# Turning 128 tokens' activations by DMA instead of on TensorE, in a fused attention and feed-forward kernel

## The chip, the cores and the metric

The kernel runs on one core of one Trainium2 chip. A core has five engines that run their own instruction lists side by side: PE (TensorE, matrix products into PSUM), DVE (VectorE), ACT (ScalarE), POOL (GpSimd) and SP (SyncE, which here only issues transfers). Sixteen DMA engines move data between HBM and the on-chip memory SBUF. The metric is device time of one execution in microseconds (us), as the median of several runs.

## The reference

Eight batches, twelve heads, 448 tokens, head size 64; the attention has no softmax, and its output is the input of a two-layer network with squared ReLU:

```python
scores = scale * np.matmul(q, k.transpose(0, 1, 3, 2))
attn = np.maximum(scores, 0.0) ** 2 / S
x = np.matmul(attn, v)          # rearranged to 3584 tokens x 768
h = x @ w_in                    # 768 -> 2048
g = np.maximum(h, 0.0) ** 2
out = g @ w_out                 # 2048 -> 768
```

## The kernel before

Everything on the chip is in fp16, with fp32 sums in PSUM. The attention is cut into 24 units (8 batches, 3 groups of 4 heads). Per unit and 64-key round, PE makes scores (L525), DVE or ACT takes the ReLU out of PSUM (`rel`, L541 on DVE, L544 on ACT), ACT or POOL squares it (`at`, L548 and L551), and PE multiplies by v (`av`, L591). When a batch's three units are done, the attention output stands turned in `xt` (L611, L613), and PE multiplies it by w_in (L653): the result `h` comes with the hidden features on the partitions, so that its square, `g` (ACT L642, masked by DVE L637), can be the stationary operand of the products with w_out (L873).

The products with w_out are a two-by-two Strassen scheme (`o_groups`): two chunks of 128 tokens, and the two halves of w_out in both directions, give seven products of eight matmuls instead of eight. It needs sums of g (`s1` to `s4`, buffers `comb`, DVE L852), sums of w_out (`t1` to `t4`, buffers `wt` and one of `w`, DVE L839), and partial results (`part`: copies by ACT L793 or DVE L795, closing sums by DVE L885, then stores by SP, L749). In the order of the code the seven are called m1, m2, m6, m5, m7, m3, m4. m1 and m2 read g itself, of the first chunk; m6 needs s2 and t2; m5 needs s1 and t1; m4 reads g of the second chunk. s2 is made from s1, and t2 from t1.

The first batch is started early, in two parts: its first 128 tokens, then the other 320. For the first 128 (`h_first`), PE multiplies the other way round (L702, four groups of six matmuls, one for each quarter of w_in as it arrives), so that the result has the tokens on the partitions. ACT squares (L715) and DVE masks it (L710) into two `comb` buffers. Then, twice, eight PE transposes (L729) turn it into PSUM, and a copy by ACT or DVE (L732) brings it into `g`. The tokens 0 to 127 of batch 0 are `chunk(0, 0)`; they are paired with `chunk(0, 1)` in the first seven products, while `chunk(0, 2)` waits for `chunk(1, 0)` of the next batch.

Loads: POOL issues w_in (L499), v (L492), the first q and k (L409) and w_out (L504); SP issues the later q and k (`raw`, L392), each held back by a one-element POOL memset (L389) on its buffer. From the seventh unit on, q and k are cast by POOL (L443) and turned by transposing DMAs from SP (L479); before that, PE turns them (L463, copies L466).

No order is written down. Each operation is given to a planner (`Plan`) with its cost on each engine that could do it, its inputs, its buffers and a due time; the planner plays the program through with those costs, tries a few rules, keeps the order that ends first by its own reckoning, and emits the instructions of each engine in that order. `after` holds an operation back in the planner's time alone: on the chip an engine goes on as soon as its semaphores allow. While PE has nothing ready before planner time 45, the planner gives it dummy matmuls (L1023) to keep it busy. A POOL operation that follows one of the L839 or L852 operations in the plan waits for it.

The lines that place the work around the change:

```python
work += [(0.2157 * NM, wide(z, 2 * two + z)) for z in range(2)]
work.append((0.057 * NH, turn))
...
new = o_groups(chunk(0, 0), chunk(0, 1))
push([(0.0, combine_w2)])
...
new = o_groups(chunk(b - 1, 2), chunk(b, 0))
```

Of the kernel before, what the change touches and what calls it, by code (L numbers as in the profile page):

```python
# [11 lines left out]
FP16 = mybir.dt.float16  # L12
# [288 lines left out]
def kernel(  # L301
# [9 lines left out]
    nc = tc.nc  # L311
# [7 lines left out]
    P = 128  # L319
# [6 lines left out]
    NH = NF // 2  # L326
# [7 lines left out]
    sb = ctx.enter_context(tc.tile_pool(name="sb", bufs=1))  # L334
    psum = ctx.enter_context(tc.tile_pool(name="ps", bufs=1, space=bass.MemoryType.PSUM))

    def fixed(pool, name, n, shape, dt):
        return [pool.tile(shape, dt, name=f"{name}{i}", tag=f"{name}{i}") for i in range(n)]
# [4 lines left out]
    ident = sb.tile([P, P], FP16, name="ident", tag="ident")  # L343
# [6 lines left out]
        "xt": fixed(sb, "xt", 2, [P, NM, S], FP16),  # L350
        "g": fixed(sb, "g", 2, [P, NF, S], FP16),
        "rest": fixed(sb, "rest", 2, [P, NF, P], FP16),
        "comb": fixed(sb, "comb", 6, [P, NH, P], FP16),
        "part": fixed(sb, "part", 6, [P, HALF], FP32),
        "rel": fixed(sb, "rel", 8, [P, 512], FP32),
        "mm": fixed(psum, "mm", 8, [P, 512], FP32),
# [1 line left out]
    plan = Plan(pools, {"PE": 5.0, "ACT": 0.7, "DVE": 1.2, "POOL": 1.4, "SP": 0.7})  # L358
# [10 lines left out]
    def act(n, emit):  # L369
        return "ACT", 0.09 + 0.00081 * n, 0.187 + 0.00081 * n, emit  # L370

    def dve(n, emit):
        return "DVE", 0.07 + 0.001045 * n, 0.149 + 0.001045 * n, emit
# [135 lines left out]
    PARTS = slice(0, 2 * TP), slice(2 * TP, S)  # L509
# [150 lines left out]
    def h_group(b, f):  # L660
        def run():
            gts.setdefault(b, Buf("g"))
            bank = Buf("mm")
            op = plan.pe(0.1892 * NM, h_mms(bank, b, f, WHOLE, 0),
                         xt_ops[b, 0] + [w1_ops[f // 4]], [bank, xts[b]])
            evac_g(op, bank, b, [f], WHOLE)
        return 0.1892 * NM, run

    def h_part(fs, cols):

        w = cols.stop - cols.start
        cost = max(0.098, 0.000424 * w) * NM
        cell: list = []

        def block(z):
            def run():
                gts.setdefault(0, Buf("g"))
                if not z:
                    cell.append(Buf("mm"))
                op = plan.pe(cost, h_mms(cell[0], 0, fs[z], cols, z * w),  # L680
                             xt_ops[0, cols.start] + [w1_ops[fs[z] // 4]] + cell[1:],
                             [cell[0], xts[0]])
                cell.append(op)
                if z == len(fs) - 1:
                    evac_g(op, cell[0], 0, fs, cols)
            return run

        return [(cost, block(z)) for z in range(len(fs))]

    def h_first():  # L690

        work = []
        for two in range(2):
            buf, marks = Buf("comb"), []

            def wide(z, i, buf=buf, marks=marks):
                def run():
                    bank = Buf("mm")

                    def emit():  # L700
                        for m in range(NM):
                            nc.tensor.matmul(  # L702
                                bank.tile, lhsT=xts[0].tile[:, m, PARTS[0]], rhs=w1[i][:, m, :],
                                start=(m == 0), stop=(m == NM - 1), skip_group_check=True)

                    def dst():
                        return buf.tile[:, 4 * z:4 * z + 4].rearrange("p f c -> p (f c)")

                    def mask():
                        nc.vector.scalar_tensor_tensor(  # L710
                            out=dst(), in0=bank.tile, scalar=0.0, in1=dst(), op0=ALU.is_gt,
                            op1=ALU.mult)

                    op = plan.pe(0.2157 * NM, emit, xt_ops[0, 0] + [w1_ops[i]], [bank, xts[0]])
                    one = plan.add([act(512, lambda: nc.scalar.activation(  # L715
                        out=dst(), in_=bank.tile, func=AF.Square))], [op], [bank, buf],
                        due=plan.now + 0.3)
                    marks.append(plan.add([dve(512, mask)], [one], [bank, buf],
                                          due=plan.now + 0.9))
                return run  # L720

            def turn(two=two, buf=buf, marks=marks):
                gts.setdefault(0, Buf("g"))
                ps, g = Buf("mm"), gts[0]

                def flip():
                    flat = ps.tile.bitcast(FP16)
                    for f in range(NH):
                        nc.tensor.transpose(flat[:, f * P:(f + 1) * P], buf.tile[:, f], ident)  # L729

                def copy(fn):
                    return lambda: fn(  # L732
                        g.tile[:, NH * two:NH * two + NH, PARTS[0]],
                        ps.tile.bitcast(FP16).rearrange("p (f c) -> p f c", c=P))

                op = plan.pe(0.057 * NH, flip, list(marks), [ps, buf])
                done = plan.add(
                    [("DVE", 0.62, 0.7, copy(nc.vector.tensor_copy)),
                     ("ACT", 0.93, 1.02, copy(nc.scalar.copy))], [op], [ps, g],
                    due=plan.now + 0.3)  # L740
                g_ops.setdefault(0, []).append((done, two, PARTS[0]))

            work += [(0.2157 * NM, wide(z, 2 * two + z)) for z in range(2)]
            work.append((0.057 * NH, turn))
        return work

# [15 lines left out]
    def filled(b, half, cols):  # L762

        return [op for op, h, c in g_ops[b]
                if half in (None, h) and c.start < cols.stop and cols.start < c.stop]
# [13 lines left out]
    def chunk(b, c):  # L779
        cols = slice(c * P, (c + 1) * P)  # L780
        return (lambda half=None: filled(b, half, cols), lambda: gts[b], lambda: gts[b].tile[:, :, cols],
                [(b, 2 * c), (b, 2 * c + 1)])

    def rest_chunk(pr):
        return (lambda half=None: rests[pr][0], lambda: rests[pr][1], lambda: rests[pr][1].tile,
                [(2 * pr, TJ - 1), (2 * pr + 1, TJ - 1)])
# [151 lines left out]
    def push(work):  # L938
        nonlocal queued
        for c, fn in work:  # L940
            fifo.append((c, fn))
            queued += c
# [13 lines left out]
    def push_dense(b):  # L956
        if b:
            hs = [h_group(b, f) for f in range(NF)]
        else:
            hs = [z for f in range(NF) for z in h_part([f], PARTS[1])]  # L960
        if b == 0:
            if PLAIN0:
                both = [plain_groups(chunk(b, c)) for c in range(2)]
                new = [both[c][hf] for hf in range(2) for c in range(2)]
            else:
                new = o_groups(chunk(0, 0), chunk(0, 1))
                push([(0.0, combine_w2)])
        elif b % 2 == 0:
            new = o_groups(chunk(b, 0), chunk(b, 1))
        else:  # L970
            pr = b // 2
            new = o_groups(chunk(b - 1, 2), chunk(b, 0))
            if pr % 2 == 1:
                new += o_groups(rest_chunk(pr - 1), rest_chunk(pr))
            new += o_groups(chunk(b, 1), chunk(b, 2))
        old = backlog[:QUOTA[b]]
        beside = max(0, len(old) - 2)
        done = 0
        for i, g in enumerate(hs):
            push([g])  # L980
            upto = (i + 1) * beside // len(hs)
            push(old[done:upto])
            done = upto
        if b == 0:
            push([(0.0, lambda: None)])
        if b % 2 == 1:
            push([(0.0, lambda: rest(b // 2))])
        push(old[done:])
        backlog[:] = backlog[len(old):] + new
        now = QUOTA[b] - len(old)  # L990
        push(backlog[:now])
        del backlog[:now]
        if b == 0 and PLAIN0:
            push([(0.0, combine_w2)])

    ORDER = "u3 v3 u4 v4 u5 v5 w0 w2 w3 w1"
    EARLY = 6
    PLAIN0 = False
    NPE = 6
    FIRST = (((21,), None), ((22, 23), None), ((24, 25), None), ((26, 27), None), ((28, 29), None),  # L1000
             (range(30, 34), 3), ((34, 35), None), ((36, 37), None), (range(38, 42), 4))
# [104 lines left out]
    for w_ in "kq":  # L1106
        turn_pe(3, w_, casts[3, w_])
    some_h(NF)
    push_dense(0)

    def coming(n):
# [10 lines left out]
    for steps, done in bursts():  # L1122
        now = steps[0] if steps else ROUNDS
        for n in range(NU, NUN):
# [6 lines left out]
            if n > 3 and reached("turn", n, TJ * (n - 1) - 5):  # L1131
                if n >= EARLY:
                    for w in "kq":
                        casts[n, w] = cast_qk(n, w, raws[n, w])
                if n < NPE:
                    for w in "kq":
# [22 lines left out]
        if done is not None and done % NU == NU - 1:  # L1159
            push_dense(done // NU)  # L1160
# [36 lines left out]
```

## Time and profile before

| | us |
|---|---|
| median of 13 runs | 379.31 (378.05 to 381.95) |
| the profiled execution | 379.53 |
| its span, first to last instruction | 377.8 |
| PE busy in the span | 367.0 |
| DVE, ACT, POOL busy | 272.7, 269.4, 221.0 |

The span leaves 1.73 us of the execution's time around it. Times in the profile count from the start of the span. A line such as "PE mm L653" is the group of PE instructions of line 653 of the kernel that write the buffers `mm`. "Busy" for PE contains modelled ends of pipelined matmuls, so neighbouring pieces overlap a little; in the chain of waits the pieces follow each other without overlap, and they are the ones to add up.

### The profile page before, as it was taken

The numbers are of one execution on the slowest core, as the hardware profiler recorded it, in microseconds if no ns is written. First come the engines' busy times: TensorE is split into PE (matmuls) and PEld (weight loads), VectorE is DVE, ScalarE is ACT, GpSimd is POOL, SyncE is SP. The second block draws the span as 40 slices with busy tenths as digits, with TensorE's granted clock in tenths as the row PEclk, the third lists the DMA queues.
The fourth block names the chain that finished last, engine by engine and source line by source line (L and its number), as shares of the span: only waits on it lengthen the run. The fifth ranks groups of instructions, "written<-read, shape, count | busy, mean of one in ns | idle before, by whom it ended". The sixth has DMA issues, their size and how long they took to land.

```text
span 377.8 us, 8786 instructions
## 1 busy us (share of the span) xinstructions
PE 367.0 (97%) x3277; PEld 196.6 (52%) x3277; DVE 272.7 (72%) x472; ACT 269.4 (71%) x587; POOL 221.0 (58%) x271
## 2 busy tenths in 40 slices
PE   7789999999999999999999999999999999999995
PEld 3545555454455445545555555545555555555663
DVE  2985899968966777677977666868777687366631
ACT  5998999869976898688767678677867675243221
POOL 7999975668766777666486457856575433000100
PEclk9999999999999999999999999999999999999999
DMA  8999998498589582981578873774643002200243
GB/s 182 194 208 203 203 233 225 126 173 244 110 192 237 161 183 51 225 165 26 144 136 196 197 177 72 184 172 85 155 81 95 3 13 51 61 24 0 64 104 84
DMA packets 70218, 51.36 MB, mean 136 GB/s; under 512 B 36896, under 2 KB 70176, under 8 KB 70176
## 3 DMA queue, kind: packets, MB, share of 16 engines
q1 hardware_dynamic: 52384, 35.86, 37.8%
q0 software_dynamic: 16928, 14.09, 25.0%
q10 hardware_dynamic: 864, 0.85, 0.7%
q8 instruction: 25, 0.41, 0.4%
q14 instruction: 17, 0.14, 0.1%
HBM read 45.61 MB, written 11.01 MB: 150 GB/s over the span
## 4 chain that ended last, share of the span: by engine, by line
PE 90%; DMA 5%; ACT 2%; POOL 1%; DVE 1%; issue 1%; ACTq 0%; POOLq 0%
PE mm L653 38%; PE mm L873 33%; PE mm L525 9%; PE mm L591 7%; DMA w<-in_moe_w_in_dram 3%; DMA g<-in_k_dram 2%; ACT at L548 1%; PE mm L463 1%; PE mm L702 1%; POOL comb L551 1%; ACT rel L544 0%; ACT part L793 0%; POOL vs L492 0%; DVE rel L541 0%; DVE part L885 0%
## 5 line engine op out<-in xcount | busy, mean ns | idle before, releaser
L551 POOL TENSOR_TENSOR at<-rel 128x448 f16<-128x448 f32 (+1 forms) x148 | 134.0, 928 | 69.8 <-DVE rel L541 52.2
L653 PE MATMUL mm<-xt,w 128*128 128x448 f16 (+1 forms) x768 | 147.8, 346 | 0.0
L637 DVE SCALAR_TENSOR_TENSOR g<-mm,g 128x448 f16<-128x448 f32 (+1 forms) x128 | 76.9, 604 | 46.4 <-ACT g L642 46.1
L653 PEld LDWEIGHTS <-w 128*128 128x128 f16 x768 | 73.0, 98 | 68.0 <-issue 7.4
L642 ACT ACTIVATE g<-mm 128x448 f16<-128x448 f32 (+1 forms) x128 | 69.6, 545 | 49.8 <-PE mm L653 49.4
L541 DVE TENSOR_SCALAR rel<-mm 128x448 f32<-128x448 f32 (+3 forms) x172 | 94.6, 592 | 12.0 <-PE mm L525 10.8
L548 ACT ACTIVATE at<-rel 128x448 f16<-128x448 f32 (+1 forms) x188 | 98.9, 593 | 0.4 <-DVE rel L541 0.3
L544 ACT ACTIVATE rel<-mm 128x448 f32<-128x448 f32 (+2 forms) x176 | 84.9, 557 | 4.6 <-PE mm L525 4.6
L873 PEld LDWEIGHTS <-comb 128*128 128x128 f16 x448 | 42.0, 98 | 33.4 <-issue 5.5
L525 PE MATMUL mm<-qkt,qkt 64*64 64x448 f16 (+2 forms) x756 | 49.3, 336 | 0.9 <-DVE rel L541 0.4
L885 DVE SCALAR_TENSOR_TENSOR part<-mm,part 128x384 f32<-128x384 f32 x56 | 30.5, 553 | 24.9 <-ACT part L793 13.4
L793 ACT ACTIVATE part<-mm 128x384 f32<-128x384 f32 x42 | 21.1, 505 | 35.3 <-PE mm L873 34.6
L443 POOL CAST blk<-raw 128x896 f16<-128x896 f32 x36 | 33.3, 931 | 19.6 <-DVE wt L839 6.5
L873 PE MATMUL mm<-w,comb 128*128 128x384 f16 x224 | 39.8, 327 | 0.0
L873 PE MATMUL mm<-wt,comb 128*128 128x384 f16 x224 | 39.6, 327 | 0.0
L873 PEld LDWEIGHTS <-g 128*128 128x128 f16 x288 | 27.6, 98 | 20.6 <-issue 2.5
L591 PE MATMUL mm<-at,vs 64*64 64x448 f16 (+1 forms) x672 | 35.2, 344 | 0.1
L873 PE MATMUL mm<-w,g 128*128 128x384 f16 x192 | 33.9, 326 | 0.3 <-DVE rel L541 0.3
L525 PEld LDWEIGHTS <-qkt 64*64 64x64 f16 x756 | 18.8, 105 | 23.9 <-issue 18.9
L492 POOL DMA_DIRECT2D vs<-in_v_dram x48 | 29.8, 629 | 2.1 <-DMA g<-in_k_dram 1.4
L774 POOL COPY rest<-g 128x1024 f16<-128x1024 f16 x8 | 8.4, 1050 | 36.0 <-DVE comb L852 35.2
L591 PEld LDWEIGHTS <-vs 64*64 64x64 f16 x756 | 21.6, 107 | 14.8 <-issue 3.7
(59 smaller groups left out, 197.9 us busy)
## 6 DMA issues: line engine op xcount, KB each, us to landing
out_dram<-part SPq DMA_DIRECT2D x108, 96.0 KB, 2.2
raw<-in_k_dram SPq DMA_DIRECT2D x18, 448.0 KB, 4.3
raw<-in_q_dram SPq DMA_DIRECT2D x18, 448.0 KB, 4.8
vs<-in_v_dram POOLq DMA_DIRECT2D x48, 112.0 KB, 4.4
w<-in_moe_w_in_dram POOLq DMA_DIRECT2D x4, 768.0 KB, 12.7
w<-in_moe_w_out_dram POOLq DMA_DIRECT2D x4, 768.0 KB, 13.5
g<-in_k_dram POOLq DMA_DIRECT2D x4, 224.0 KB, 11.2
g<-in_q_dram POOLq DMA_DIRECT2D x4, 224.0 KB, 10.2
```

The lines of the kernel that those rows point to most:

```text
L443: return lambda: fn(blk.tile.rearrange("p t (f d) -> p f t d", f=2), tile_of().rearrange("p f (t d) -> p f t d", d=D))
L525: nc.tensor.matmul(sp[e].tile[64 * c:64 * c + 64, c0:c0 + w].rearrange("p (t c) -> p t c", c=TP), lhsT=kT[r, t, 64 * e:64 * e + 64], rhs=q ...
L541: dve(width, lambda: nc.vector.tensor_scalar(out=r.tile[:, 0:width], in0=bank.tile[:, 0:width], scalar1=0.0, scalar2=SK, op0=ALU.max, op1= ...
L544: act(width, lambda: nc.scalar.activation(out=r.tile[:, 0:width], in_=bank.tile[:, 0:width], func=AF.Relu, scale=SK))],
L548: act(width, lambda: nc.scalar.activation(out=dst(), in_=r.tile[:, 0:width], func=AF.Square)),
L551: lambda: nc.gpsimd.tensor_mul(dst(), r.tile[:, 0:width], r.tile[:, 0:width]))],
L591: nc.tensor.matmul(banks[f].tile[64 * e:64 * e + 64, c0:c0 + w], lhsT=vs[r, e ^ c, t * D:(t + 1) * D], rhs=a[r, e, :], start=(t == 0), sto ...
L637: nc.vector.scalar_tensor_tensor(out=dst, in0=src, scalar=0.0, in1=dst, op0=ALU.is_gt, op1=ALU.mult)
L642: nc.scalar.activation(out=dst, in_=src, func=AF.Square)
L653: nc.tensor.matmul(bank.tile[:, c0:c0 + w], lhsT=w1[f // 4][:, m, f % 4 * P:(f % 4 + 1) * P], rhs=xts[b].tile[:, m, cols], start=(m == 0), ...
L873: nc.tensor.matmul(buf.tile[:, 0:HALF], lhsT=lhs()[:, j, :], rhs=w[:, j, :], start=(first and j == 0), stop=(j == NH - 1), skip_group_chec ...
L885: done = plan.add([dve(HALF, lambda: nc.vector.scalar_tensor_tensor(out=osb.tile, in0=src.tile[:, 0:HALF], scalar=sign * CO, in1=r.tile, o ...
```

## The change

`turn` no longer gives PE eight transposes and ACT or DVE a copy. It gives SP one transposing DMA, from the `comb` buffer (128 tokens x 1024 features) to its place in `g`, with a planner time of 58 or later. It is done twice. There is a seventh `comb` buffer, as two now stay in use until the DMA has read them. The pairs in w_out's products change: batch 0 pairs its chunks 1 and 2, and chunk (0, 0) is paired with (1, 0) of the next batch.

```diff
-        "comb": fixed(sb, "comb", 6, [P, NH, P], FP16),
+        "comb": fixed(sb, "comb", 7, [P, NH, P], FP16),
...
             def turn(two=two, buf=buf, marks=marks):
                 gts.setdefault(0, Buf("g"))
-                ps, g = Buf("mm"), gts[0]
-
-                def flip():
-                    flat = ps.tile.bitcast(FP16)
-                    for f in range(NH):
-                        nc.tensor.transpose(flat[:, f * P:(f + 1) * P], buf.tile[:, f], ident)
...
-                op = plan.pe(0.057 * NH, flip, list(marks), [ps, buf])
-                done = plan.add(
-                    [("DVE", 0.62, 0.7, copy(nc.vector.tensor_copy)),
-                     ("ACT", 0.93, 1.02, copy(nc.scalar.copy))], [op], [ps, g],
-                    due=plan.now + 0.3)
+                g = gts[0]
+                done = plan.add([("SP", 1.3, 5.0, lambda: nc.sync.dma_start_transpose(
+                    out=g.tile[:, NH * two:NH * two + NH, PARTS[0]],
+                    in_=buf.tile.rearrange("p f c -> p (f c)")), 690000)],
+                    list(marks), [buf, g], after=TURN_AT)
                 g_ops.setdefault(0, []).append((done, two, PARTS[0]))
...
-                new = o_groups(chunk(0, 0), chunk(0, 1))
+                new = o_groups(chunk(0, 1), chunk(0, 2))
...
-            new = o_groups(chunk(b - 1, 2), chunk(b, 0))
+            new = o_groups(chunk(b - 1, 0 if b == 1 else 2), chunk(b, 0))
...
+    TURN_AT = 58.0
```

As the planner plays the whole program through, the changed kernel also has another order on every engine until about the second batch's products with w_out; from there the PE order is the same.

More of the change, by code (lines that the diff above doesn't have):

```diff
@@ L723, in turn @@
                 gts.setdefault(0, Buf("g"))
-                ps, g = Buf("mm"), gts[0]
-                def flip():
-                    flat = ps.tile.bitcast(FP16)
-                    for f in range(NH):
[L729 to L734, printed above, removed]
-                op = plan.pe(0.057 * NH, flip, list(marks), [ps, buf])
-                done = plan.add(
-                    [("DVE", 0.62, 0.7, copy(nc.vector.tensor_copy)),
-                     ("ACT", 0.93, 1.02, copy(nc.scalar.copy))], [op], [ps, g],
-                    due=plan.now + 0.3)
+                g = gts[0]
[3 more added lines that the diff above has]
+                    list(marks), [buf, g], after=TURN_AT)
                 g_ops.setdefault(0, []).append((done, two, PARTS[0]))
```

## The prediction

> **What bounds the kernel now.** I read the page's busy shares and slices first, then the chain of waits in order of time, then the waits of PE alone, then the timeline of DVE and POOL around the first products with w_out, then the DMA issues.
>
> ```profile
> PE 367.0 (97%) x3277; PEld 196.6 (52%) x3277; DVE 272.7 (72%) x472; ACT 269.4 (71%) x587; POOL 221.0 (58%) x271
> PE   7789999999999999999999999999999999999995
> ```
> ```profile
> 28.18 0.90 ACT g L732
> ...
> 30.68 0.60 PE mm L1023 x4
> 31.28 1.45 PE mm L702 x6
> 32.72 0.51 PE mm L463 x14
> 33.23 1.08 PE mm L591 x28
> 34.31 0.51 PE mm L463 x14
> 34.82 0.55 PE mm L729 x8
> 35.38 0.81 PE mm L653 x6
> ```
> ```profile
> 58.55 0.38 PE mm L525 x8
> 58.93 6.61 PE mm L873 x40
> 65.54 1.45 PE mm L591 x28
> 66.99 1.41 PE mm L873 x8
> 68.39 0.50 PE mm L525 x8
> ```
> ```profile
> 61.47 1.21 DVE L852 TENSOR_TENSOR comb<-g 128x1024 f16<-128x1024 f16 x1
> 62.60 0.54 DVE L885 SCALAR_TENSOR_TENSOR part<-mm,part 128x384 f32<-128x384 f32 x1
> 63.07 2.40 DVE L839 TENSOR_TENSOR wt<-w,wt 128x1536 f16<-128x1536 f16 x2
> 65.39 0.68 DVE L852 TENSOR_TENSOR comb<-comb,g 128x1024 f16<-128x1024 f16 x1
> ```
> ```profile
> 62.85 0.93 POOL L551 TENSOR_TENSOR at<-rel 128x448 f16<-128x448 f32 x1
> ```
> ```profile
> PE mm L873 <- DVE rel L541: 0.3, 1, 0.3
> ```
> ```profile
> qkt<-blk SPq DMA_TRANSPOSE x36, 3.0
> ```
>
> PE is the bound from about 31 us on: from 31.28 to 98.95 the chain is PE alone, and between 85 and 125 us PE's list of waits has the single line shown. So after 31 us a change counts by what it does to PE's own list, and by whether something PE needs comes too late. Before 31 us the quarters of w_in decide: the third and fourth L702 groups start at 27.48 and 31.25, and the DMA issues of 13.3 and 14.1 us took 14.2 and 17.0 to land, which is 27.5 and 31.1.
>
> The chain gives prices. Eight L873 cost 1.30 (6.61 for 40, less 0.11), six L653 of 320 columns 0.82, four L525 0.19. Each turn between attention and dense work adds some 0.11: L525 x8 is 0.38 after L591 but 0.50 after L873, L591 1.33 after L525 but 1.45 after L873. A group of transposes after other dense work pays it too.
>
> **What the Trainium skill says.** "TensorE: Matmul & The Clock Gate", Part 4, says that a PE transpose ends in PSUM, so that a copy has to follow, and prices one at about 275 to 390 ns. The copy is here (L732, 1.03 on ACT, 0.69 on DVE), but eight transposes take 0.55 in the chain, so back to back one costs 0.06. "VectorE: DVE Perf Modes", The three transpose paths, gives 1309 ns for 128x128 by DMA; in this trace seven such blocks (L479) land 3.0 after the issue. "DMA: Bandwidth & Descriptors", Rules for kernel authors: issuing from other queues does not add bandwidth, as all run on the same 16 DMA engines. The trace agrees: after 51 us three 448 KB loads from SP and POOL's w_out loads share them, and SP's second, issued at 51.73, needs 9.0. "SBUF — State Buffer", two separate sides: POOL and a two-input DVE operation lock each other out for a whole instruction. The trace agrees: of the two L839 at 63.07, the first meets POOL's L551 (62.85 to 63.78), and the pair takes 2.40, where two alone take 1.81 (65.99).
>
> **The change part by part.** The changed program, built but not run, gives the orders below.
>
> 1. Sixteen transposes leave PE. The first eight (27.04) lie ahead of the third L702, whose weights land at 27.5: worth nothing. The second eight are worth 0.45 of work.
>
> 2. Two copies leave, 1.03 of ACT and 0.69 of DVE. The ACT copy lies on the drawn chain at 28.18, but this chain leads into dummy matmuls and then to L702 at 31.25, just when its weights land at 31.1. I take nothing. The upper end is 0.9 gained, if w_in landed that much earlier.
>
> 3. Dummy matmuls rise from 10 to 28. Ten more stand before 12 us; their delay (some 0.2) is covered by w_in's loads. Twelve instead of five stand ahead of the fourth L702. PE is through with the 28 L591 and four L525 by about 30.1; twelve at 0.11 end at 31.4, so L702 starts 0.2 later (0 to 0.5). One more costs 0.11 after it.
>
> 4. The rest of PE's list after the fourth L702 has the same work, but turns between attention and dense work rise from 104 to 110 (+0.66), and groups of transposes with a turn of their own fall from five to two, one dummy counted back (-0.2). With -0.45 from 1 and +0.11 from 3 this is +0.1. Added up group by group, the last L653 of batch 0 ends at 56.8, as before (56.72).
>
> 5. The pairing. Before, PE has m1, m2 of the first seven, m1 of the next, then m5, then m2 of the next, L591, and only then m6 (66.92). DVE, in that time, makes s1, closes m2 (L885), makes t2 and s2 (ready at 66.07). Now chunk (0, 0) comes by DMA and chunk 2 is in the first pair. PE's order is m1, L591, L525, m2, m5, m1 of the next pair, m6. DVE's is s1, L613, L541, L885 closing m2, t2, s2. DVE keeps its order, so t2 waits for the L885, and the L885 for the end of m2. From there m6 is away by 0.2 (PE to DVE) + 0.47 (L885) + 1.74 to 2.32 (t2 alone, or beside POOL) + 0.68 (s2) + 0.1 = 3.2 to 3.8. PE has two products of 1.30 to do meanwhile. It stands for 0.6 to 1.2; I take 1.0, as POOL has casts and squares there. Behind m6 queues all of PE. By group prices m2 ends at 62.1, so m6 starts near 65.8 instead of 64.7; L591, m7 and m3 behind it find t3 and s4 ready (67.5, 68.2).
>
> 6. m2 of the next pair goes to the second batch's end, ahead of twelve L525. Where PE now waits 0.34 for DVE (L541, at 99.3), it has 1.30 of work: -0.3 (0 to -0.34).
>
> 7. The two DMAs. `TURN_AT` is planner time; on the chip they follow three raw loads on SP, from about 52.5 us, while w_out's last load runs to 56.4 (issued 38.9, 17.5 to land). Each moves 256 KB; one L479 of 224 KB kept the DMA engines full from 145.50 to 146.75, so each takes about 1.3. The raw loads ahead of them landed at 57.6, 60.7 and 61.9, so the first turn should land near 63 and the second near 64.5. New waits: m1 of the next pair at 63.4 needs the first; m2 of it, at 95 or later, the second. A first turn up to 64.6 is hidden in the stall of 5, since m6 waits for DVE anyway. Should they instead hold up w_out's last quarter by 2.6, it lands at 59.0, and m2 asks for it at 60.7: nothing. On SP they issue in 2.5 to 2.8, and SP sat idle from 55.3 to 59.4. The L479 of unit 6 behind them land by 67, and its scores come at 70. The fourth raw load, now behind stores that wait for m2's closing, starts near 64 instead of 60.8, for a cast at 69 or later: covered. POOL takes over two 128-column squares ahead of one early q load, some 0.6, but that load lies 16 us in the queue.
>
> The sum: 0.2 + 0.1 + 1.0 - 0.3 = +1.0 on the profiled execution, 379.53 to 380.5. The median of the runs is 0.22 lower, so 380.3. No wait further on gives this back: PE's order is the same from batch 2 on, and PE is full to the end.
>
> **The rivals.** *The stall of step 5 does not come* (no change): if DVE runs t2 alone and PE's start of m6 is held by something that was there anyway, 0.6 to 1.0 goes away: 379.4. For it: DVE has 1.3 less to do between the last L710 and s1 (25.0 against 26.3 by the rows' means). Against: the chain through L885 starts at m2's end, however early DVE is.
>
> *Relief of ACT decides* (faster): ACT is full from 20 to 30 us, and the chain runs through its copy. If w_in lands 0.9 earlier than 31.1, PE starts its full stretch 0.9 earlier, the dummies of step 3 being then the only hindrance. With the stall at its low end this is -0.9 + 0.1 + 0.6 - 0.3 = -0.5, and with the stall gone -1.1: 378.2 to 378.8, say 378.4. It decides from a landing before 30.8. Against: those loads were 14 and 17 us in a full queue, which the change doesn't shorten.
>
> *The turned data is late* (slower still): if the first DMA lands at 66, m1 of the next pair waits 2.6, and m6 waits no more: 0.2 + 0.1 - 0.3 + 2.6 = +2.6, 381.9. For it: the 9.0 of the raw load ahead of it, and low DMA shares from 59 to 60.5, as of single engines behind the others. Against: 1.5 us of margin.
>
> That the change does not do what it says is no rival on PE: the transposes are gone from its list. Only the "behind w_out's loads" is by SP's order, not by the clock (step 7).
>
> **How the numbers follow.** Forecast 0.57; no stall 0.20; relief 0.15; late data 0.08. About 0.2%, 0.76 us, is what a measurement of this kernel can tell from no change. The forecast lies 0.26% up, with its own range of 379.6 to 381.2; three quarters and more of it is over the bound. Slower: 0.46 + 0.08 + a little of the second = 0.57; same: 0.11 + 0.15 = 0.26; faster: the relief and a little of the second, 0.17. The range of 8 in 10, 378.4 to 382.0, takes in the second case, half of the third, and the fourth; what is left out is more relief than 0.9, or a stall that comes twice.
>
> **What would show it.** L729 and L732 are gone, 28 dummies; the fourth L702 at 31.3 to 31.6; the last L653 of batch 0 at 56.8 to 57.2; in PE's waits a new one of about 1 us on DVE `comb` or `wt`, near 65 us; L885 ahead of the pair of L839 starting within 0.3 of m2's end; the gap at 99 gone. A wait of PE on a DMA into `g` would make step 7 wrong; an L702 before 31.0, step 3; no wait near 65, step 5.

## The result and the profile after

The changed kernel takes 380.53 us (median of 11 runs, 379.91 to 382.16); the kernel before, run beside it, 379.31. The ratio is 1.003, with a 95% interval of 1.0017 to 1.0042: 1.2 us slower. The profiled execution has a span of 378.6, against 377.8.

From the page after, the busy time of the engines in the span:

```profile
PE 368.7 (97%) x3279; PEld 197.2 (52%) x3279; DVE 269.4 (71%) x467; ACT 270.8 (72%) x588; POOL 222.3 (59%) x273
```

DVE has 3.3 us less to do (five instructions fewer), ACT and POOL 1.4 and 1.3 more, and PE, which is the bound, 1.7 more. DVE's lighter work bought nothing. The chain of waits after, around the fourth L702 (start, us, what):

```profile
27.49 1.46 PE mm L702 x6
28.95 1.08 PE mm L591 x28
30.02 0.14 PE mm L525 x4
30.16 1.42 PE mm L1012 x12
31.58 1.29 PE mm L702 x6
```

The third group starts where it did before (27.48). Behind it the twelve dummies run to the moment at which the fourth starts: PE was not waiting for weights there. The fourth comes 0.30 later in the chain (31.58 against 31.28).

The line numbers of the second half are twelve lower in the kernel after: L861 is a product, L873 a closing sum, L840 a sum of g, L827 a sum of w_out. PE's timeline after, from the last L653 of batch 0 (in brackets: idle before, and who ended it):

```profile
56.80 0.57 PE L525 MATMUL mm<-qkt,qkt 64*64 64x448 f16 x8
57.31 1.47 PE L861 MATMUL mm<-w,g 128*128 128x384 f16 x8
58.71 1.52 PE L591 MATMUL mm<-at,vs 64*64 64x448 f16 x28
60.06 0.55 PE L525 MATMUL mm<-qkt,qkt 64*64 64x448 f16 x8
60.54 1.47 PE L861 MATMUL mm<-w,g 128*128 128x384 f16 x8
61.85 1.46 PE L861 MATMUL mm<-wt,comb 128*128 128x384 f16 x8
63.15 1.46 PE L861 MATMUL mm<-w,g 128*128 128x384 f16 x8
65.38 1.47 PE L861 MATMUL mm<-wt,comb 128*128 128x384 f16 x8 [0.76 <-DVE comb L840]
```

The products are m1, m2, m5, m1 of the next pair (m1'), and m6. m6 is the one wait. m2 of the next pair (m2'), which stood ahead of m6 before, now follows at 98.21. DVE's timeline after, in the same stretch:

```profile
62.11 0.56 DVE L873 SCALAR_TENSOR_TENSOR part<-mm,part 128x384 f32<-128x384 f32 x1 [0.57 <-ACT rel L544]
62.58 2.13 DVE L827 TENSOR_TENSOR wt<-w,wt 128x1536 f16<-128x1536 f16 x2
64.64 0.68 DVE L840 TENSOR_TENSOR comb<-comb,g 128x1024 f16<-128x1024 f16 x1
```

DVE stands 0.57, closes m2 (L873), makes t2 (the two L827) and s2 (L840), and m6 starts as s2 ends. The profile puts the 0.57 down to ACT's L544; m2's last product ends at the same time by the model (60.54 + 1.47), so this line doesn't tell the two apart. Later, PE's list of waits after between 85 and 125 us is empty: the gap of 0.34 near 99 us is gone. The DMA issues of the stretch list the two turning DMAs with the median time from issue to landing, 7.1 us:

```profile
g<-comb SPq DMA_TRANSPOSE x2, 7.1
```

The starts of the fourth L702 differ by up to a microsecond from one execution to the next with the landing of the loads, so I compare stretches of PE's timeline instead: (a) from the third to the fourth L702, (b) from there to the end of batch 0's last L653, (c) from there to batch 1's first L653 (448 columns), (d) from there to batch 2's first L653, (e) from there to PE's end. They are starts of groups in the timeline (the end of b is a modelled end), without the first 27 us. The kernels of the experiments, which are described below, stand in the same table; m2' (1.30 of PE) lies in (c) where marked, otherwise in (d).

| kernel | median, us | ratio to before, 95% | a | b | c | d | e |
|---|---|---|---|---|---|---|---|
| before | 379.31 | | 3.77 | 25.47 | 17.23, m2' | 44.60 | 254.97 |
| after | 380.53 | 1.003 (1.0017 to 1.0042) | 3.92 | 25.46 | 17.30 | 45.45 | 254.89 |
| pairing alone | 379.04 | 0.9994 (0.9982 to 1.0006) | 3.77 | 25.47 | 17.23, m2' | 44.59 | 254.80 |
| DMA turn alone | 381.55 | 1.0052 (1.0032 to 1.0072) | 3.79 | 25.27 | 18.83, m2' | 44.99 | 254.84 |
| close later | 380.46 | 1.003 (1.0022 to 1.0038) | 3.93 | 25.46 | 17.14 | 45.45 | 254.90 |
| m6 behind L591 | 380.65 | 1.0033 (1.0022 to 1.0043) | 3.93 | 25.45 | 17.11 | 45.45 | 254.90 |
| no dummies | 380.19 | 1.0031 (1.0022 to 1.004) | 3.44 | 25.45 | 17.31 | 45.44 | 254.99 |
| both | 379.99 | 1.0024 (1.0011 to 1.0036) | 3.28 | 25.45 | 17.15 | 45.44 | 254.90 |
| m2' put back | 381.96 | 1.0077 (1.0062 to 1.0091) | 3.93 | 25.45 | 17.67, m2' | 45.29 | 254.89 |
| turn later | 385.49 | 1.016 (1.0133 to 1.0186) | 3.94 | 25.45 | 22.04 | 45.45 | 254.90 |
| turn early | 383.10 | 1.0101 (1.0085 to 1.0116) | 3.94 | 26.80 | 18.42 | 45.45 | 254.92 |
| planned at 60 | 380.33 | 1.0026 (1.0015 to 1.0037) | 4.22 | 25.28 | c + d: 63.01 | | 255.02 |
| early, planned at 54 | 384.69 | 1.0133 (1.0105 to 1.0161) | 3.84 | 27.85 | 21.81, m2' | 44.60 | 254.82 |
| the same, fewer dummies | 384.63 | 1.0138 (1.012 to 1.0156) | 3.80 | 27.55 | 21.52, m2' | 44.59 | 254.82 |

The medians are to be read against the kernel before beside the same run: 379.13 for "close later" to "both", 379.19 for the two halves, "turn later" and "planned at 60", and 379.39 for the other four.

After against before: a +0.15, b 0, c + d +0.92, e -0.08, together +1.0. Of c + d, the new wait at m6 is 0.76 of idle PE, and the gap that went 0.34. From start to start they are worth a little more: m6 starts at 65.38, 0.93 behind the place where m1' lets it (63.15 + 1.30), and before, the product behind the gap started at 99.61, 0.40 behind the place where twelve L525 let it (98.51 + 0.70). PE's list has two more turns between attention and dense work in c and none in d, 0.22 at 0.11 each. That leaves some 0.2 of the 0.92 that no line here accounts for.

The table leaves out the time ahead of the third L702. In one execution of each kernel, that group starts at 27.08 to 27.63 in the eight kernels with after's order up to there, which has fifteen dummies ahead of 12 us, and at 26.54 to 27.48 in the six that have five to ten. The kernel before (27.48) and the pairing alone (26.75), with five each, are themselves 0.7 apart. So a part of the loss may lie in these dummies; no run takes them out, and it stays open.

### The profile page after: what moved, and what is told of

The parts are those of the page before. It is cut to its first block, busy times and chain, and to the rows that moved or that the text cites. A ratio compares the mean times of both kernels' runs of the same rounds, so it can differ in the third digit from the quotient of the medians.

```text
span 378.6 us, 8769 instructions
## 1 busy us (share of the span) xinstructions
PE 368.7 (97%) x3279; PEld 197.2 (52%) x3279; DVE 269.4 (71%) x467; ACT 270.8 (72%) x588; POOL 222.3 (59%) x273
## 4 chain that ended last, share of the span: by engine, by line
PE 90%; ACT 3%; DVE 2%; DMA 2%; issue 1%; POOL 0%; ACTq 0%; DVEq 0%; POOLq 0%
PE mm L653 37%; PE mm L861 33%; PE mm L525 9%; PE mm L591 8%; DMA g<-in_k_dram 2%; ACT rel L544 1%; PE mm L702 1%; PE mm L463 1%; ACT at L548 1%; DVE rel L541 1%; PE mm L1012 1%; ACT comb L548 1%; DVE wt L827 1%; DVE part L873 0%; ACT g L642 0%
## 5 line engine op out<-in xcount | busy, mean ns | idle before, releaser
L653 PE MATMUL mm<-xt,w 128*128 128x448 f16 (+1 forms) x768 | 147.9, 346 | 0.0
L653 PEld LDWEIGHTS <-w 128*128 128x128 f16 x768 | 73.0, 98 | 68.5 <-issue 7.7
L541 DVE TENSOR_SCALAR rel<-mm 128x448 f32<-128x448 f32 (+3 forms) x169 | 93.2, 592 | 12.9 <-PE mm L525 12.0
L548 ACT ACTIVATE at<-rel 128x448 f16<-128x448 f32 (+1 forms) x188 | 98.1, 590 | 0.0
L544 ACT ACTIVATE rel<-mm 128x448 f32<-128x448 f32 (+2 forms) x179 | 85.8, 552 | 7.6 <-PE mm L525 7.3
L861 PEld LDWEIGHTS <-comb 128*128 128x128 f16 x448 | 42.1, 98 | 34.3 <-issue 5.8
L873 DVE SCALAR_TENSOR_TENSOR part<-mm,part 128x384 f32<-128x384 f32 x56 | 30.6, 554 | 30.3 <-ACT part L781 17.8
L525 PE MATMUL mm<-qkt,qkt 64*64 64x448 f16 (+2 forms) x756 | 49.9, 341 | 0.9 <-DVE rel L541 0.4
L861 PE MATMUL mm<-wt,comb 128*128 128x384 f16 x224 | 39.6, 326 | 0.8 <-DVE comb L840 0.8
L861 PE MATMUL mm<-w,comb 128*128 128x384 f16 x224 | 39.8, 327 | 0.0
L861 PEld LDWEIGHTS <-g 128*128 128x128 f16 x288 | 27.4, 98 | 21.0 <-issue 3.2
L591 PE MATMUL mm<-at,vs 64*64 64x448 f16 (+1 forms) x672 | 35.2, 344 | 0.0
L861 PE MATMUL mm<-w,g 128*128 128x384 f16 x192 | 34.0, 326 | 0.0
L525 PEld LDWEIGHTS <-qkt 64*64 64x64 f16 x756 | 18.6, 107 | 24.1 <-issue 19.3
L591 PEld LDWEIGHTS <-vs 64*64 64x64 f16 x756 | 21.9, 110 | 14.9 <-issue 3.4
```

The costliest lines, as they stand in the source:

```text
L525: nc.tensor.matmul(sp[e].tile[64 * c:64 * c + 64, c0:c0 + w].rearrange("p (t c) -> p t c", c=TP), lhsT=kT[r, t, 64 * e:64 * e + 64], rhs=q ...
L541: dve(width, lambda: nc.vector.tensor_scalar(out=r.tile[:, 0:width], in0=bank.tile[:, 0:width], scalar1=0.0, scalar2=SK, op0=ALU.max, op1= ...
L544: act(width, lambda: nc.scalar.activation(out=r.tile[:, 0:width], in_=bank.tile[:, 0:width], func=AF.Relu, scale=SK))],
L548: act(width, lambda: nc.scalar.activation(out=dst(), in_=r.tile[:, 0:width], func=AF.Square)),
L591: nc.tensor.matmul(banks[f].tile[64 * e:64 * e + 64, c0:c0 + w], lhsT=vs[r, e ^ c, t * D:(t + 1) * D], rhs=a[r, e, :], start=(t == 0), sto ...
L653: nc.tensor.matmul(bank.tile[:, c0:c0 + w], lhsT=w1[f // 4][:, m, f % 4 * P:(f % 4 + 1) * P], rhs=xts[b].tile[:, m, cols], start=(m == 0), ...
```

## The experiments

The kernels keep the planner's order and change it afterwards, by its numbers of operations: `behind(i, j)` moves operation i of the issuing order behind operation j. Where only the planner's inputs are changed, it plans anew.

**The close of m2 later.** m2's closing sum (433) and its stores go behind s2 (427).

```diff
+        behind(433, 427)
+        behind(434, 433)
+        behind(435, 434)
```

> The kernel after, with one VectorE instruction and its two stores later in the order: L873, which closes the second product, stands behind t2 and s2 instead of ahead of t2. Theory (the new pairing leaves PE only two products to do between the second product's end and m6, and VectorE's order ties t2 to that end): t2 starts as soon as s1 and the copies ahead of it are done, s2 is ready before PE asks for it, PE's wait of 0.76 us at m6 is gone, and the time falls by 0.6 to 0.9 us, to 379.6 to 379.9 beside after's 380.5. Rival A (VectorE as a whole is short of time there, so that what is moved only moves the wait): the wait comes back at L591 or at the next product, time within 0.2 us of after. Rival B (the 1.2 us that after lost do not come from this wait but from the clock and loads): the wait is gone and the time stays within 0.2 us.

DVE's timeline of this kernel, where L842 is t2 and L855 a sum of g:

```profile
61.51 3.09 DVE L842 TENSOR_TENSOR wt<-w,wt 128x1536 f16<-128x1536 f16 x2
64.52 0.68 DVE L855 TENSOR_TENSOR comb<-comb,g 128x1024 f16<-128x1024 f16 x1
```

And POOL's:

```profile
59.91 2.27 POOL L458 CAST blk<-raw 128x896 f16<-128x896 f32 x2
62.15 1.63 POOL L566 TENSOR_TENSOR at<-rel 128x448 f16<-128x448 f32 x1
```

t2 starts 1.07 earlier than after and ends 0.12 earlier, because the pair takes 3.09 instead of 2.13: it now meets POOL's second cast and then its square, where after it met the end of the square alone. The wait at m6 falls from 0.76 to 0.60, and the time doesn't change. My theory is refuted: without the L873 ahead of it, s2 is ready only 0.12 earlier. Rival A has it right that the wait stays and the time too; that DVE is held by POOL in this stretch is read from the two timelines, and not tested by a run of its own. This is the exclusive port that the Trainium skill describes ("SBUF — State Buffer", SBUF: two separate sides: a DVE operation with two SBUF inputs and a POOL operation that reads SBUF shut each other out for a whole instruction). The trace agrees: two such additions take 1.81 where POOL is silent, and 3.09 here; POOL's own square takes 1.63 instead of 0.92.

**m6 behind L591.** PE's m6 (459) behind the 28 L591 (446).

```diff
+        behind(459, 446)
```

> The kernel after, with TensorE's m6 behind the group of 28 L591 that follows it, VectorE untouched. Theory (PE stands at m6 for VectorE's s2, and has other work at hand): PE does the 28 L591 in the 1.45 us in which s2 is made; the wait of 0.76 us shrinks to what ScalarE's last casts (L548, until about 65.4 us) leave, 0 to 0.5 us, and the time falls by 0.3 to 0.8 us. Rival A (ScalarE is just as late as VectorE): L591 waits as long as m6 did, time within 0.2 us of after. Rival B (clock and loads, not this wait): no wait, and no change of the time.

PE's timeline of this kernel:

```profile
64.65 1.52 PE L604 MATMUL mm<-at,vs 64*64 64x448 f16 x28
66.10 1.47 PE L874 MATMUL mm<-wt,comb 128*128 128x384 f16 x8
68.16 1.46 PE L874 MATMUL mm<-w,comb 128*128 128x384 f16 x8 [0.58 <-ACT part L794]
```

L591 and m6 run without a wait; the next product, m7, waits 0.58 for ACT's copy of m6's result (L794), since it goes on in the same bank. With L591 moved ahead, nothing stands between m6 and m7 any more. The stretch c is 0.19 shorter, and the median is not: rival A has the time right. The wait moved by one product, which neither theory had named.

**No dummies ahead of the fourth L702.** The dummies between place 200 of the order and the fourth L702 (215) are left out, twelve products that carry no result.

```diff
+        last = next(z for z, (_, op) in enumerate(self.order) if op is not None and op.id == 215)
+        self.order[200:last] = [x for x in self.order[200:last] if x[1] is not None]
```

> The kernel after without the twelve dummy products (L1012) ahead of the fourth L702; they carry no result. Theory (twelve dummies of 0.12 us are longer than the gap that they stand in, so that they hold up L702 by 0.3 us): L702 starts when its weights have landed, at 31.1 to 31.3 us instead of 31.58, and the time falls by 0.3 to 0.4 us. Rival (the dummies keep PE's clock up, or the weights of w_in land at 31.5 anyway): L702 starts no earlier, or the matmuls behind it are slower; time equal to after's or up to 1 us longer.

Third to fourth L702 is 3.44 instead of 3.92, so the trace shows 0.48 gained. L702 now waits for the attention output that DVE copies, which the dummies had covered:

```profile
PE mm L707 <- DVE xt L618: 0.8, 1, 0.8
```

It is not held by its weights, and the products behind it are no slower without the dummies (b is 25.45 against 25.46), so neither half of the rival is seen. The ratio to before, 1.0031, doesn't tell this kernel from after, and the medians lie 1.06 and 1.22 over the kernel before. The trace speaks for the theory in this stretch; the runs leave open how much of the 0.48 is kept.

**Both.** The first and the third edit together.

> The kernel after with both edits: L873's close behind s2 on VectorE, and the twelve dummies ahead of the fourth L702 left out. Theory (the wait at m6 and the dummies are two losses in series on PE, 0.76 and 0.3 us): they add up, time down by 0.9 to 1.2 us, to 379.3 to 379.6 us, level with the kernel before. Rival (one of them only hides the other, or PE is held by loads): time falls by no more than the larger of the two alone.

Stretches a and c add up to 0.8 less than after's, but the median lies 0.86 over the kernel before, against 1.22, with overlapping intervals: 0.36 less, where 0.9 to 1.2 was expected, and still slower than before. Two edits at the places that look guilty don't undo the change.

**The two halves of the change.** The pairing alone, with PE's transposes kept; and the DMA turn alone, with the old pairing. Both are planned anew. For the first, against the kernel before:

```diff
-                new = o_groups(chunk(0, 0), chunk(0, 1))
+                new = o_groups(chunk(0, 1), chunk(0, 2))
...
-            new = o_groups(chunk(b - 1, 2), chunk(b, 0))
+            new = o_groups(chunk(b - 1, 0 if b == 1 else 2), chunk(b, 0))
```

> The kernel before with the new pairing alone: chunk (0, 0)'s products stand with batch 1's, but its g is turned by TensorE and copied out of PSUM as before; the planner orders the rest anew (10 dummies and 102 turns between attention and dense work, as before). Theory (the pairing makes the wait at m6): PE waits 0.5 to 1.2 us at m6 in the first products, and 0.34 us near 99 us is gone; time +0.3 to +0.8 us against before, 379.6 to 380.1. Rival A (the loss of after comes from the turn by DMA, from its traffic and its order): time within 0.2 us of before. Rival B (the planner's order alone decides, by chance): another wait than that at m6 is found, time anywhere between -1 and +1 us.

For the second, the same lines turned back in the kernel after.

> The kernel before with the turn by DMA alone: the first 128 tokens' g of batch 0 is turned behind w_out's loads, but its products stay paired as before; 14 dummies, 97 turns between attention and dense work against 102. Theory (what is taken off PE is 0.45 us of transposes and some turns of 0.11 us; the data lands near 62 us and holds up the products only if the old pairing asks for it before): if the first products wait for DMA until 62 us, PE has to be given other work or waits 1 to 4 us, time +1 to +4 us; where the planner finds other work, time -0.3 to -1.0 us. Rival (the turn by DMA has a cost of its own through the loads beside it): time +0.5 us or more although no product waits for it.

The pairing alone costs nothing: 0.9994, with 1 inside the interval, and every stretch equals before's to 0.01, e aside. My theory is wrong again, and rival A holds. PE's timeline of the pairing alone:

```profile
58.13 4.07 PE L873 MATMUL mm<-w,g 128*128 128x384 f16 x24
62.05 1.46 PE L873 MATMUL mm<-wt,comb 128*128 128x384 f16 x8
63.34 1.46 PE L873 MATMUL mm<-w,g 128*128 128x384 f16 x8
64.74 1.52 PE L591 MATMUL mm<-at,vs 64*64 64x448 f16 x28
66.19 1.47 PE L873 MATMUL mm<-wt,comb 128*128 128x384 f16 x8
```

Three products read g at once (m1, m2 and m1'), then m5, then m2', then L591, and only then m6. From the close of m2 on, DVE has the same list here as in the kernel after (close at 61.87, t2 at 62.34, s2 from 64.66 to 65.34), but behind m5 PE has m2' and L591 to do ahead of m6, and comes to it at 66.19, when s2 has been ready for 0.85. With g early, the planner puts m1' and m2' ahead of m6; told that the turned g comes after 58, it puts m1' behind m5 and m2' at the end of the second batch.

The DMA turn alone costs 2.0 (0.52% of 379.3, with an interval of 1.2 to 2.7), and no product of it waits for the DMA. PE's waits of that kernel between 31 and 130 us (sum, times, longest):

```profile
PE mm L653 <- DVE part L873: 0.8, 1, 0.8
PE mm L591 <- DVE part L873: 0.5, 1, 0.5
PE mm L653 <- ACT rel L544: 0.4, 1, 0.4
PE mm L861 <- DVE rel L541: 0.3, 1, 0.3
```

These are 2.0 of waits for other engines, where before has 0.3 in the same stretch; the stretches a to e add up to 1.7 more than before's. Both numbers of the theory were wrong: not the wait for DMA and not the gain. The rival's sign came (0.5 or more, and no product waiting for the turn), though through waits for DVE and ACT; loads that come late are not seen here. So the turn, with the order that the planner makes for it, costs 2.0, the pairing costs nothing, and both together 1.2. That the pairing takes back 0.8 of it is not clear of the noise, as the two intervals overlap. The order of one plan could be bad luck; but all three orders made for a turn behind w_out's loads (this one, after, and the one planned at 60 below) are slower than the kernel before.

**m2' back to its place.** In the kernel after, m2' (624) behind m1' (622), with a free PSUM bank; its close (625) and stores (626, 627) move along.

```diff
+        tile_of(624, "mm").tile = tile_of(432, "mm").tile
+        tile_of(626, "part").tile = tile_of(623, "part").tile
+        behind(624, 622)
+        behind(625, 247)
+        behind(626, 396)
+        behind(627, 626)
```

> The kernel after with the next pair's second product (m2', eight L861) put back where the kernel before has it: behind m1' and ahead of m6, instead of the second batch's end near 99 us; its close and stores move along. Theory (the wait at m6 is not made by VectorE's order but by PE being 1.30 us short of work in this stage, since the turned data keeps m2' out of it): no wait at m6; from the last L653 of batch 0 to batch 1's first L653 17.7 to 18.0 us, with m2' in it (after 17.30 without it, before 17.23 with it), and from there to the next batch's L653 44.6 to 44.9 instead of 45.45; time 0.2 to 0.5 us below after. Rival (VectorE, GpSimd and ScalarE bound the stage, whatever PE has to do): a wait comes back at m6, L591 or m7, the stage takes 18.3 us or more, time equal to after's or longer.

The wait at m6 is gone and c is 17.67, as the theory says, and m2' has no wait for the DMA: it was the plan, and not the landing on the chip, that kept it from here. But d is 45.29, not 44.6 to 44.9. PE's waits of this kernel from 56 to 130 us:

```profile
PE mm L548 <- DVE g L660: 0.9, 1, 0.9
```

The last scores ahead of the second batch's products (L548) wait 0.91 for a PSUM bank that DVE empties. m2' had covered a hole there in the kernel after. So this one product fills either the hole at m6 (0.76) or the hole at 99 us (0.91 here, 0.34 in before), and the other stays open. The stretches add up to 0.2 more than after's; the median lies 2.6 over before's, against 1.2. The profiled execution was the shortest of its six (380.83; the others 381.75 to 383.27), and no trace of a longer one is there, so the rest of that loss stays open. That PE was short of work at m6 is shown by this run; that this is what the change lost is not, as the time didn't come back.

**Where the turn is issued.** Later: both DMAs behind the two L479 on SP. Early: both right after the masks that they wait for.

```diff
+        behind(168, 328)
+        behind(223, 168)
```

```diff
+        behind(168, 217)
+        behind(223, 168)
```

> The kernel after with the two turning DMAs (L725) behind the two L479 on SyncE's queue instead of ahead of them. Theory (the turned data is hidden in after with a margin of about 1.5 us, and a turn takes 5 to 8 us to land): it lands near 66 to 67 us, m1 of the pair waits 2.5 to 4 us for it, time +2 to +4 us. Rival (issued behind the raw loads, they take less time, since the loads are through): landing by 64.5, wait under 1 us, time +0 to +1 us.

> The kernel after with the two turning DMAs (L725) first on SyncE's queue, right after the masks near 35 us, beside w_out's loads; all else in after's order. Theory (where in the queue they stand costs nothing, the order that the late landing forced costs 1.2 us): data lands by 45 us, same waits as after, time within 0.2 us of after's. Rival A (issued behind the raw loads they hold up SyncE for 7.5 us, and that is part of the loss): time 0.3 us or more below after. Rival B (beside w_out's loads they delay w_out's last quarter): the second product or the sums t1, t2 start later, time 0.3 us or more above after.

Later, PE's one wait between 31 and 130 us is

```profile
PE mm L875 <- DMA g<-comb: 4.0, 1, 4.0
```

m1' waits 4.05 for the DMA and starts at 66.96; c grows by 4.74, and the median lies 6.3 over before's, against 1.2. That is more than the 2 to 4 expected: SP came to the L479 at 60.89 and to the turn at 63.61. The theory of a thin margin holds.

Early: PE's waits from 31 to 85 us are

```profile
PE mm L875 <- DMA w<-in_moe_w_out_dram: 1.4, 1, 1.4
PE mm L477 <- DMA g<-in_k_dram: 0.6, 1, 0.6
PE mm L477 <- DMA raw<-in_k_dram: 0.6, 1, 0.6
PE mm L875 <- DVE comb L854: 0.4, 1, 0.4
```

Three loads come late, those of k for the attention and w_out for m2; b grows by 1.34 and c by 1.12. Rival B is right, with 3.7 over before's median against 1.2. In after the DMA engines are full from 30 to 50 us, and the transfer put among the loads there made those behind it later. This is what the Trainium skill says of the 16 DMA engines that all queues share ("DMA: Bandwidth & Descriptors", Rules for kernel authors), and the trace agrees: from 30 to 50 us POOL's queue moved 3.35 MB (1.62 + 1.73) instead of 4.02 (2.00 + 2.02), while SP's moved 0.52.

**Other orders of the planner.** `TURN_AT` 60 instead of 58:

> The kernel after with one number changed: the planner is told that the turning DMAs start at 60 us, not 58; its order then has 14 dummies and 99 turns between attention and dense work, against 28 and 108. Theory (dummies ahead of the fourth L702 cost 0.3 us and each turn some 0.11 us, both being chance of the order and not of the idea): time 0.5 to 1.3 us below after, if the order makes no new wait. Rival A (turns are worth nothing, the profile's 0.11 us being an effect of the waits): time within 0.3 us of after. Rival B (the turns start later on the chip, so that the pair's product waits for its data): PE waits 1 us or more for DMA near 63 us, time +0.5 us or more.

The order has 14 dummies fewer and, by the planner's count, 9 turns between attention and dense work fewer, and the ratio, 1.0026, is not to be told from after's. PE waits 0.9 and 0.3 at the products in place of 0.76, and a is 4.22. Rival A's number came out, but not shown for its reason: the waits changed together with the turns, so this run doesn't say what a turn is worth.

`TURN_AT` 54, with the DMAs early; and the same with the dummies behind place 200 of the order left out:

```diff
-    TURN_AT = 58.0
+    TURN_AT = 54.0
...
+        behind(168, 217)
+        behind(223, 168)
```

> The kernel after with the turning DMAs right after the masks as in the run that turns early, and with the planner told that they start at 54 us: its order for PE is then that of the kernel with the new pairing alone, without the sixteen transposes and with eight dummies more (18, and 102 turns). Theory (the turn by DMA costs only through the order that a late landing forces): no wait at m6, 17.2 us from the last L653 of batch 0 to batch 1's first L653, 44.6 from there to the next; the transposes' 0.55 us come off PE against 0.3 of dummies; time 0.1 to 0.4 us below before, 378.8 to 379.1. Rival (the transfers themselves, or the dummies, cost something): time equal to before's or up to 1 us above it.

> The same kernel as the early turn with the planner's 54 us, without the dummy products (L1012) from the fourth L702 on backwards to the first 20 us: eight of the eighteen go; they carry no result. Theory (dummies of 0.11 us each, which stand ahead of work that is ready, delay it): third to fourth L702 3.3 to 3.5 us instead of 3.77 in before, and 0.2 more behind it; time 0.5 to 0.9 us below before, 378.3 to 378.7. Rival (the fourth L702 waits for its weights, or PE's clock falls without dummies): time within 0.2 us of the same kernel with them.

PE's order from the products on is that of the pairing alone, and there d is 44.60, as expected. But the early transfers push the loads again: m2 waits 2.7 for w_out, the attention 1.6 and 0.7 for k, and the time is 5.3 above before. Without eight dummies it is the same, 384.63, since the fourth L702 then waits for w_in's last quarter. The longest wait of the first kernel, and this one of the second:

```profile
PE mm L875 <- DMA w<-in_moe_w_out_dram: 2.7, 1, 2.7
```

```profile
PE mm L717 <- DMA w<-in_moe_w_in_dram: 1.0, 1, 1.0
```

The rival of the second expectation holds, in its first half. No kernel here beats the one before; the pairing alone equals it. The order of the pairing alone with the turn left behind w_out's loads wasn't tried: m1' would ask near 60.7 for data that lands near 62.

## The prediction, point by point

The time said was 380.3, the time measured is 380.53. The wait at m6 and the gap that goes came at their places and near their sizes, and the sum of +1.0 is the sum of the stretches. The forecast was read off the changed kernel's own order, and so the numbers came; the reason given for the largest one, the pairing, failed when the pairing was run alone. That the total agrees to 0.2 is partly luck: some 0.2 of c and d has no term in it, and the wait was smaller than said.

- *Steps 1 and 2, transposes and copies, worth nothing ahead of the fourth L702.* As said: the third L702 starts at 27.49, against 27.48, in the two profiled executions. Behind the fourth, stretch b is equal to 0.01: the 0.45 of the second transposes is taken up by four more turns between attention and dense work, 0.44 at 0.11 each, and one dummy, less what the transposes' own turns gave.
- *Step 3, twelve dummies, 0.2 later.* Measured 0.15 between the starts of the third and the fourth L702, 0.30 in the chain; without them 0.48 less than after. That the ten dummies ahead of 12 us cost nothing is not tested.
- *Step 4, +0.1 for the turns.* The last L653 of batch 0 ended at 56.87 (said 56.8). Behind it came two more turns, the 0.2 that I had counted. Some 0.2 in c and d stays without a term.
- *Step 5, "the pairing", a wait of 1.0 at m6 near 65.8.* The wait came at m6, 0.76 of idle PE (0.93 from start to start), ending at 65.38. Its cause as I put it failed twice. The pairing alone has no wait and costs nothing. And the link from m2's end through L885 to t2 doesn't decide: with the close behind s2 the wait is 0.60, as the additions then take 3.09 beside POOL's cast and square. In its place the runs showed this: the plan made for a late turn takes m2' out of the place where PE needs work, so PE comes to m6 before s2 is ready. With m2' put back that wait is gone. With L591 put ahead instead, PE stops one product later, at ACT's copy. The time came back in neither run, so what the whole 1.2 consists of is only in part shown.
- *Step 6, -0.3 at 99 us.* The gap of 0.34 is gone. It is not a gain of its own: it is the other side of the same product m2', as the run that puts it back has a wait of 0.91 there.
- *Step 7, DMA hidden, first landing near 63.* SP needed 3.9 for the first issue, and 7.5 for both in place of the 2.5 to 2.8 said; the first still landed at 61.7 (53.11 + 8.6), the second by about 62.6. No wait for them. The remark that a delay of w_out's last quarter by 2.6 costs nothing holds in the place where the change put them, as m2 has no wait for w_out; some 20 us earlier the medians lie 2.5 further over before's.
- *The rivals.* No relief of ACT, no late data. "The stall does not come" would have needed what the run with m6 behind L591 has, and there the wait only moved.

## What to carry to other kernels

When data is made cheaper but arrives later, look at which work of the bound engine the plan then moves away: here one product of 1.30 left its place, and a wait of 0.76 stood there, more than the 0.45 of transposes saved. Undo the parts of a change one at a time before believing the part that looks guilty in the timeline: the wait stood in a product of the new pairing, but the pairing alone had no wait and lost no time. When several engines are nearly full in one stretch, taking away the wait that is seen may only show the next one: from 58 to 67 us DVE was busy for 8.43 of the 9 us and ACT for 8.24, and each run that moved work there kept most of the wait or met another one.

## What the runs showed of the hardware

In these runs a transposing DMA that SP issued behind its own plain loads held SP for longer. SP's timeline after:

```profile
52.66 0.40 SPq L392 DMA_DIRECT2D raw<-in_k_dram  x1
53.11 3.94 SPq L725 DMA_TRANSPOSE g<-comb  x1
```

and in the kernel that turns later, when those loads have landed:

```profile
63.61 2.68 SPq L739 DMA_TRANSPOSE g<-comb  x2
```

There one takes 1.34 to issue and lands 3.2 after; behind three loads of 448 KB one takes 3.8 (7.52 for two) and lands 7.1 after in the median. Beside POOL's full queue alone, in the early run, the issue of the second took 1.28, but both landed 10.7 after in the median. And the early turn displaced more than it moved: 0.67 MB less on POOL's queue for 0.52 MB on SP's from 30 to 50 us.
